# Moving the second half of m's preparation to later items, on ScalarE, VectorE and TensorE, in an attention, soft-MoE and squared-ReLU kernel

## The chip, the cores and the metric

The kernel is one program on one core of a Trainium2 chip. The metric is the device time of one execution in microseconds (us); lower is better. Times are given as the median of several executions, and one further execution is profiled, which gives the trace.

## The reference, cut to what matters

Three layers run one after the other: a chunked attention, a soft mixture of experts, and a feed-forward layer with a squared ReLU. The change lies in the last one. The output of the second layer is a product of a (3072 x 32) softmax matrix c and a (32 x 512) matrix slot_out, so the first product of the third layer can be taken as c @ (slot_out @ w_in): the small matrix m = slot_out @ w_in is computed first, and h = c @ m.

```
logits = x @ phi                               # x: 3072 x 512, phi: 512 x 32
c = softmax(logits, axis=1)
x2 = c @ slot_out                              # slot_out: 32 x 512
h = x2 @ w_in                                  # w_in: 512 x 2048, so h = c @ m, m = slot_out @ w_in
r = max(h, 0)
g = s * (r * r) + b
out = g @ w_out                                # w_out: 2048 x 512
```

## The kernel before, in words

**Items.** In the third layer the work is cut into 128 items. An item is one pair of a block of 384 rows (b) and a slice of 128 hidden columns (f). For one item TensorE computes h for the slice (`emit_h`, one 128x384 product of `cpack` with 128 columns of `mpack`, a PSUM tile of tag `s`), ScalarE applies the ReLU (L825), squares it (L829) and rounds it to a high part `ghi` (L833), VectorE takes the rest as a low part `glo` (L836), and TensorE multiplies both by the slice of w_out: six products of 512 columns with `whi` (`emit_o`, L871) and three with `wlo` (`emit_o2`, L883), which are summed in PSUM over the slices of a run. Items 0 to 15 are slices 0 to 7 of row blocks 0 and 1 in turn; items 16 to 47 are slices 0 to 15 of blocks 2 and 3 in turn. At the end of a run the sums are moved out of PSUM by L888 on ScalarE and L890 on VectorE, and the next run's first product into each of these tiles waits for that.

**Weights.** Every second item up to 46 also converts one piece of a weight (a "key", the number of the item it belongs to): ScalarE L573, then VectorE L583, L585, L587, L594, and for pieces of w_out ScalarE L792 (`whi`) and VectorE L785 and L787 (`wlo`).

**m.** `mpack` holds m in four groups of 512 columns, four slices each; its upper 64 rows are the high half, its lower 64 rows the low half. Group 0 is made ahead of the items. Groups 1, 2 and 3 are made beside items 4, 26 and 34 (`M_AT`): `emit_m` multiplies parts of slot_out by a piece of w_in (L800) and ScalarE copies the four partial sums into `mps` (L802). `emit_m2`, one item later, sums the four groups of rows with one product with `stks_all` (L806, tile `mr`, tag `s`), and `m_split` makes the two halves: ScalarE casts `mr` into `mpack` (L811), then VectorE subtracts and overwrites the low half (L812). Group 1 is first read by the h of item 8, group 2 by item 32, group 3 by item 40.

**Order.** All orders are written out by hand. The loop goes over items n; its body is, for TensorE, the h of item n, the `emit_o` of item n - 3 and the `emit_o2` of item n - 4, and only for n = 5, 6 and 7 the h stands behind these two. So the h of item 7 and the h of item 8 follow each other directly. Each engine works through its own list in order. PSUM tiles of tag `s` have two buffers, for h, for `emit_m`'s partial sums and for `mr` alike; `r2` has two, `ghi` and `glo` five.

Of the kernel before, what the change touches and what calls it, by code (L numbers as in the profile page):

```python
# [35 lines left out]
def kernel(  # L36
# [11 lines left out]
    nc = tc.nc  # L48
# [18 lines left out]
    def psum(tag, shape):  # L67
        bufs = {"s": 2, "g": 2}.get(tag, 1)
        return ps.tile(shape, F32, tag=tag, name=tag, bufs=bufs)
# [48 lines left out]
    with tc.manual_schedule():  # L118
# [447 lines left out]
        def wi_dst(t, key):  # L566
            j = key[2]
            return t[j % 2][:, :, 256 * (j // 2):256 * (j // 2) + 256]
# [6 lines left out]
        def cv_dve(key, j):  # L575
            h, lf, a, w = cv[key]
            H = w[:, :, 1]
            hi, ai = h.bitcast(I32), a.bitcast(I32)
            if key[0] == "i" and key[1] > 1 and j:
                ai = wi_dst(wis_b if key[1] % 2 else wis_a, key).bitcast(I32)  # L580
                hi, H = (x.rearrange("p (k f) -> p k f", k=2) for x in (hi, H))
            if j == 0:
                nc.vector.tensor_scalar(out=hi, in0=hi, scalar1=3, scalar2=None, op0=ALU.logical_shift_left)  # L583
            elif j == 1:
                nc.vector.scalar_tensor_tensor(out=ai, in0=H, scalar=SIGN, in1=hi, op0=ALU.bitwise_and, op1=ALU.bitwise_or)  # L585
            else:
                nc.vector.tensor_scalar(out=hi, in0=ai, scalar1=EXPM, scalar2=None, op0=ALU.bitwise_and)  # L587

        def cv_low(key, out):
            h, lf, a, w = cv[key]  # L590
            low = w[:, :, 0].bitcast(U32)
            if key[0] == "i":
                low, h = (x.rearrange("p (k f) -> p k f", k=2) for x in (low, h))
            nc.vector.scalar_tensor_tensor(out=out, in0=low, scalar=2.0 ** -52, in1=h, op0=ALU.mult, op1=ALU.mult)  # L594
# [117 lines left out]
        for i in range(16):  # L712
            emit_w2(i)
            if i == 4:
# [3 lines left out]
                mpack = pk_p.tile([128, 128 * NF], F32R, name="mpack")  # L718
# [21 lines left out]
        M_AT = (4, 26, 34)  # L740
# [24 lines left out]
        h_t, o_t = {}, {}  # L765

        def stage_a(k):
            key = cq.get(k)
            if key:
                if key[0] == "i":  # L770
                    w = wi_src(key[1], key[2])
                else:
                    w = wt[raw_of[key]].rearrange("p (f d t) -> p f d t", f=2, t=2)[:, key[1] % 2]
                cv_act(key, k // 2 % 2, w)

        def stage_d(k, j):
            key = cq.get(k)
            if key:
                h, lf, a, w = cv[key]
                if j < 3:  # L780
                    cv_dve(key, j)
                elif j == 3:
                    cv_low(key, lf if key[0] == "o" else wi_dst([wis_l[:, 0:2], wis_l[:, 2:4]], key))
                elif key[0] == "o" and j == 4:
                    nc.vector.tensor_tensor(out=a, in0=a, in1=w_hi[key[1]].bitcast(F32), op=ALU.subtract)  # L785
                elif key[0] == "o":
                    nc.vector.tensor_tensor(out=w_lo[key[1]], in0=a, in1=lf, op=ALU.add)  # L787
# [16 lines left out]
        def emit_m2(fb):  # L804
            mr = psum("s", [128, 512])
            nc.tensor.matmul(out=mr, lhsT=stks_all, rhs=mps, start=True, stop=True)  # L806
            m_split(mr, 512 * fb, slice(0, 512))

        def m_split(mp, base, cols):
            m = mpack[:, base + cols.start:base + cols.stop]  # L810
            nc.scalar.copy(out=m, in_=mp[:, cols])  # L811
            nc.vector.tensor_tensor(out=m[64:128], in0=mp[64:128, cols], in1=m[64:128].bitcast(F32), op=ALU.subtract)  # L812

        def emit_h(n):
            if n >= len(items):
                return
            (b, _, _), f = items[n]
            hq = psum("s", [128, UT])
            nc.tensor.matmul(out=hq, lhsT=mpack[:, 128 * f:128 * f + 128], rhs=cpack[:, b * UT:(b + 1) * UT],  # L819
                             start=True, stop=True)  # L820
            h_t[n] = hq

        def emit_relu(n):
            if n < len(items):
                nc.scalar.activation(out=r_g[n % 2], in_=h_t.pop(n), func=AF.Relu)  # L825

        def emit_sq(n):
            if n < len(items):
                nc.scalar.activation(out=r2_g[n % 2], in_=r_g[n % 2], func=AF.Square)  # L829

        def emit_ghi(n):
            if n < len(items):
                nc.scalar.copy(out=ghi_g[n % (LA + 2)], in_=r2_g[n % 2])  # L833
# [28 lines left out]
        def emit_o(n, parts=(0, 1)):  # L862
            r_, f = items[n]
            ghi, glo = ghi_g[n % (LA + 2)], glo_g[n % (LA + 2)]
            if f == r_[1] and 0 in parts:
                o_t[r_] = [psum(("pt", "x", "xt", "lp", "g", "g")[3 * place[r_] + t], [128, DM]) for t in range(NTU)]
            if n == len(items) - 1:
                return
            for gt in [(ghi, glo)[x] for x in parts]:
                for t in range(NTU):  # L870
                    nc.tensor.matmul(out=o_t[r_][t], lhsT=gt[:, 128 * t:128 * t + 128], rhs=w_hi[f],  # L871
                                     start=(f == r_[1] and gt is ghi), stop=False)

        def emit_o2(n):
            r_, f = items[n]
            b, f0, f1 = r_
            ghi, glo = ghi_g[n % (LA + 2)], glo_g[n % (LA + 2)]
            for t in range(NTU):
                o = o_t[r_][t]
                if n == len(items) - 1:  # L880
                    for gt in (ghi, glo):
                        nc.tensor.matmul(out=o, lhsT=gt[:, 128 * t:128 * t + 128], rhs=w_hi[f], start=False, stop=False)
                nc.tensor.matmul(out=o, lhsT=ghi[:, 128 * t:128 * t + 128], rhs=w_lo[f], start=False, stop=(f == f1 - 1))  # L883
                if f == f1 - 1:
                    if b < 4 and f0 == 0:
                        to = part[b][t] if b < 2 else os_early(b - 2, t)
                        if t == 1:
                            nc.scalar.activation(out=to, in_=o, func=AF.Copy, scale=sbt[:, 0:1])  # L888
                        else:
                            nc.vector.tensor_scalar(out=to, in0=o, scalar1=sbt[:, 0:1], scalar2=None, op0=ALU.mult)  # L890
                    else:
                        os_ = os_g[t]
                        nc.vector.scalar_tensor_tensor(out=os_, in0=o, scalar=sbt[:, 0:1], in1=part[b][t] if f0 else bias,
                                                       op0=ALU.mult, op1=ALU.add)
                        store(b, t, os_)
# [12 lines left out]
        def stages(n, *js):  # L908
            for j in js:
                stage_d(n, j)  # L910
# [44 lines left out]
        for n in range(LA + 1, len(items) + LA + 1):  # L955
            if n > 7:
                emit_h(n)
            m = n - LA - 1
            ends = 0 <= m and items[m][1] == items[m][0][2] - 1
            late = m + 1 < len(items) and m + 1 == 2 * HF + 1  # L960
            if ends or late:
                emit_o2(m)
            if 1 < m + 1 < len(items):
                emit_o(m + 1)
            if m > 1 and not ends and not late:
                emit_o2(m)
            if LA + 1 < n <= 7:
                emit_h(n)
            if n == 6:
                nc.vector.tensor_copy(out=soTb, in_=soT4[:, :, 0, :])  # L970
            emit_relu(n)
            emit_sq(n)
            stage_a(n + 1)
            emit_ghi(n)
            if n in M_AT:
                emit_m(M_AT.index(n) + 1)
            if n - 1 in M_AT:
                emit_m2(M_AT.index(n - 1) + 1)
            if LA + 1 < n <= len(items):
                emit_g(n - 1)  # L980
            stage_d(n, 1)
            stage_w(n)
            stages(n, 2, 3)
            stages(n - 1, 4, 5)
            stage_d(n + 1, 0)
            if 48 <= n < 64:
                for i in (2 * n - 96, 2 * n - 95):
                    wsum_add(i)
            if n == 64:
                colsum()  # L990
            if 65 <= n < 77:
                add_bias(n - 65)
            while wnext[0] < len(order) and last_use.get(order[wnext[0] - NRG], -1) <= n:
                load_w(1)
# [72 lines left out]
```

## Time and profile before

| | |
|---|---|
| median of 3 runs | 477.76 us (477.14 to 479.54) |
| profiled execution, its own time | 480.6 us |
| its span, first to last instruction | 478.8 us |
| mean granted TensorE clock | 0.993 |
| busy: TensorE (PE), VectorE (DVE), ScalarE (ACT) | 456.4, 308.9, 308.5 us |

Busy shares are means over very different stages. The third layer runs from about 171 us to the end, and a row of a stretch of it says more than the share over the span. In rows of a timeline, a number in brackets at the end is the idle time of that engine just before the row and what ended it.

### The profile page before, as it was taken

Reading aid. Unit: us, or ns where it says so; the run is one execution under the profiler, and the core shown is the slowest. Engines: PE = TensorE matmul, PEld = TensorE weight load, DVE = VectorE, ACT = ScalarE, POOL = GpSimd, SP = SyncE. Lnnn points to the kernel's source line nnn. Section 1 sums busy time; section 2 is a strip of 40 time slices with the busy share of each in tenths; the row PEclk is TensorE's granted clock in tenths of the full one; section 3 lists DMA queues with packets and bytes.
Section 4 is the critical chain, followed back from the end, with each engine's and each line's share of the span. In section 5 each row is a group of like instructions: output and inputs, shape, how many; then the busy total and the mean of one; then the engine's idle time right before and its main releaser. Section 6 shows DMA issues by size and latency. Waiting matters only on the chain.

```text
span 478.8 us, 10197 instructions
## 1 busy us (share of the span) xinstructions
PE 456.4 (95%) x3960; PEld 342.6 (72%) x3960; DVE 308.9 (65%) x682; ACT 308.5 (64%) x637; POOL 84.1 (18%) x154
## 2 busy tenths in 40 slices
PE   6799999999997998999999999999999999999996
PEld 5566666665543565886787888888888888888885
DVE  6778888886486767998495999975524223223232
ACT  4566666665133477998686888665766666666660
POOL 6666565550000000000000000007700000000000
PEclk8999999999998999999999999999999999999999
DMA  8999999999999932342332000003101001001011
GB/s 302 371 408 406 406 410 403 401 377 400 374 413 376 422 133 88 114 152 94 123 136 88 1 1 0 1 0 134 67 0 67 0 1 66 0 1 65 2 66 66
DMA packets 20432, 83.04 MB, mean 173 GB/s; under 512 B 2720, under 2 KB 2848, under 8 KB 14368
## 3 DMA queue, kind: packets, MB, share of 16 engines
q1 hardware_dynamic: 20384, 82.39, 44.5%
q8 instruction: 31, 0.51, 0.4%
q14 instruction: 17, 0.14, 0.1%
HBM read 76.09 MB, written 6.29 MB: 172 GB/s over the span
## 4 chain that ended last, share of the span: by engine, by line
PE 68%; DMA 12%; DVE 11%; ACT 4%; issue 2%; SPq 1%; POOL 0%; DVEq 0%; ACTq 0%; POOLq 0%
PE g L871 11%; PE lp L871 5%; PE pt L871 5%; PE x L871 5%; PE g L883 5%; PE xt L871 5%; DMA vals<-in_vm_dram 4%; DMA keys<-in_kq_dram 4%; PE s L819 4%; PE s L624 3%; PE lp L883 3%; PE pt L883 3%; PE xt L883 3%; PE x L883 3%; PE x L319 2%
## 5 line engine op out<-in xcount | busy, mean ns | idle before, releaser
L836 DVE TENSOR_TENSOR glo<-r,ghi 128x384 fp32r<-128x384 f32 x128 | 76.3, 600 | 81.5 <-ACT ghi L833 81.3
L825 ACT ACTIVATE r<-s 128x384 f32<-128x384 f32 x128 | 62.6, 489 | 51.6 <-PE s L819 51.3
L829 ACT ACTIVATE r<-r 128x384 f32<-128x384 f32 x128 | 67.2, 525 | 10.3 <-DVE glo L836 6.4
L833 ACT CAST ghi<-r 128x384 fp32r<-128x384 f32 x128 | 65.4, 511 | 3.4
L819 PE MATMUL s<-cpack,mpack 128*128 128x384 f32 x128 | 44.6, 351 | 0.2 <-DVE mpack L812 0.2
L295 ACT ACTIVATE seg<-seg 128x384 f32<-128x384 f32 x32 | 28.8, 901 | 18.9 <-DVE seg L306 15.4
L883 PE MATMUL g<-wlo,ghi 128*128 128x512 f32 x128 | 40.2, 394 | 0.0
L871 PE MATMUL g<-whi,ghi 128*128 128x512 f32 x126 | 39.6, 394 | 0.0
L871 PE MATMUL g<-whi,glo 128*128 128x512 f32 x126 | 39.4, 393 | 0.0
L858 POOL TENSOR_TENSOR keys<-keys,bias 128x512 f32<-128x512 f32 x6 | 8.4, 1434 | 165.1 <-DVE bias L847 165.1
L257 POOL TENSOR_SCALAR keys<-keys 64x416 f32<-64x416 f32 x63 | 33.6, 534 | 12.1 <-DMA keys<-in_kq_dram 5.2
L279 PE MATMUL s<-keys 128*32 128x128 f32 x768 | 29.4, 285 | 5.6 <-POOL keys L261 4.5
L319 PE MATMUL x<-vals,seg 128*32 128x128 f32 x744 | 28.3, 275 | 3.1 <-DMA vals<-in_vm_dram 2.2
L319 PEld LDWEIGHTS x<-vals,seg 128*32 128x32 f32 x744 | 20.6, 109 | 13.2 <-DVE seg L303 4.5
L819 PEld LDWEIGHTS s<-cpack,mpack 128*128 128x128 f32 x128 | 23.9, 188 | 7.9 <-issue 1.5
L883 PEld LDWEIGHTS g<-wlo,ghi 128*128 128x128 f32 x128 | 24.0, 188 | 5.2
L871 PEld LDWEIGHTS g<-whi,glo 128*128 128x128 f32 x126 | 23.7, 188 | 5.4
L279 PEld LDWEIGHTS s<-keys 128*32 128x32 f32 x768 | 19.0, 112 | 11.4 <-POOL keys L261 6.8
L313 ACT COPY seg<-pt 128x384 f32<-128x384 f32 x32 | 15.2, 475 | 18.6 <-PE pt L311 17.7
L871 PEld LDWEIGHTS g<-whi,ghi 128*128 128x128 f32 x126 | 23.7, 188 | 4.0 <-DVE vals L890 0.4
L871 PE MATMUL lp<-whi,ghi 128*128 128x512 f32 x63 | 25.5, 404 | 0.8 <-DVE vals L890 0.8
L871 PE MATMUL pt<-whi,glo 128*128 128x512 f32 x64 | 25.3, 395 | 0.7 <-DVE glo L836 0.7
(248 smaller groups left out, 991.9 us busy)
## 6 DMA issues: line engine op xcount, KB each, us to landing
seg<-in_w_dram SPq DMA_DIRECT2D x28, 1024.0 KB, 8.9
keys<-in_kq_dram SPq DMA_DIRECT2D x32, 396.0 KB, 7.4
vals<-in_vm_dram SPq DMA_DIRECT2D x64, 192.0 KB, 6.7
keys<-in_w_in_dram SPq DMA_DIRECT2D x5, 1024.0 KB, 5.0
keys<-in_w_out_dram SPq DMA_DIRECT2D x5, 1024.0 KB, 4.9
out_dram<-os SPq DMA_DIRECT2D x18, 256.0 KB, 2.1
vals<-in_w_in_dram SPq DMA_DIRECT2D x3, 1024.0 KB, 7.8
vals<-in_w_out_dram SPq DMA_DIRECT2D x3, 1024.0 KB, 4.8
```

What stands on the lines that cost most here:

```text
L257: (nc.vector if h and u == 0 else nc.gpsimd).tensor_scalar(out=stream(kz[rows, h], 0, CH), in0=k[rows, UT * h:UT * h + (NCU + 1) * CH].rea ...
L279: nc.tensor.matmul(out=o, lhsT=qt[:, 32 * c:32 * c + 32], rhs=kz[:, :, at:at + WIN], start=True, stop=not (first or last))
L295: nc.scalar.activation(out=p_r[u], in_=sm_r[u].rearrange("p t h (a r) -> p t r (h a)", a=2), func=AF.Exp, scale=scale)
L313: nc.scalar.copy(out=pts_r[u], in_=pt)
L319: nc.tensor.matmul(out=xp[32 * r:32 * r + 32, t], lhsT=pts_r[u][:, 32 * c:32 * c + 32], rhs=vbuf[u // 2 % 2][:, u % 2, :, 64 * c:64 * c + ...
L819: nc.tensor.matmul(out=hq, lhsT=mpack[:, 128 * f:128 * f + 128], rhs=cpack[:, b * UT:(b + 1) * UT], start=True, stop=True)
L825: nc.scalar.activation(out=r_g[n % 2], in_=h_t.pop(n), func=AF.Relu)
L829: nc.scalar.activation(out=r2_g[n % 2], in_=r_g[n % 2], func=AF.Square)
L833: nc.scalar.copy(out=ghi_g[n % (LA + 2)], in_=r2_g[n % 2])
L836: nc.vector.tensor_tensor(out=glo_g[n % (LA + 2)], in0=r2_g[n % 2], in1=ghi_g[n % (LA + 2)].bitcast(F32), op=ALU.subtract)
L871: nc.tensor.matmul(out=o_t[r_][t], lhsT=gt[:, 128 * t:128 * t + 128], rhs=w_hi[f], start=(f == r_[1] and gt is ghi), stop=False)
L883: nc.tensor.matmul(out=o, lhsT=ghi[:, 128 * t:128 * t + 128], rhs=w_lo[f], start=False, stop=(f == f1 - 1))
```

## The change

`emit_m2` is called two items after `emit_m` instead of one. It no longer calls VectorE: `m_split` is cut in two, `m_high` (ScalarE) stays with `emit_m2`, and `m_low` (VectorE) is called a further item later, at the end of the loop body, behind the first conversion step of the next key (`stage_d(n + 1, 0)`, L583). So `emit_m2` stands at items 6, 28 and 36 and VectorE's part at the ends of items 7, 29 and 37. The number of instructions on each engine is the same.

```diff
         def emit_m2(fb):
             mr = psum("s", [128, 512])
             nc.tensor.matmul(out=mr, lhsT=stks_all, rhs=mps, start=True, stop=True)
-            m_split(mr, 512 * fb, slice(0, 512))
+            m_high(mr, 512 * fb, slice(0, 512))
+            h_t["m", fb] = mr
+
+        def m_high(mp, base, cols):
+            nc.scalar.copy(out=mpack[:, base + cols.start:base + cols.stop], in_=mp[:, cols])
 
         def m_split(mp, base, cols):
+            m_high(mp, base, cols)
+            m_low(mp, base, cols)
+
+        def m_low(mp, base, cols):
             m = mpack[:, base + cols.start:base + cols.stop]
-            nc.scalar.copy(out=m, in_=mp[:, cols])
             nc.vector.tensor_tensor(out=m[64:128], in0=mp[64:128, cols], in1=m[64:128].bitcast(F32), op=ALU.subtract)
...
-            if n - 1 in M_AT:
-                emit_m2(M_AT.index(n - 1) + 1)
+            if n - 2 in M_AT:
+                emit_m2(M_AT.index(n - 2) + 1)
...
             stage_d(n + 1, 0)
+            if n - 3 in M_AT:
+                fb = M_AT.index(n - 3) + 1
+                m_low(h_t.pop(("m", fb)), 512 * fb, slice(0, 512))
```

In the rows that follow, numbers at a name tell buffers apart, and what stands in square brackets are the engines whose signal an instruction waits for. The lines behind the changed functions count 7 higher in the changed kernel (L812 is L819 there, L819 is L826, L836 is L843, L871 is L878, L883 is L890).

VectorE at items 4 to 7, before; the L812 is that of m's group 1, `glo4` is item 4's:

```order
L594 SCALAR_TENSOR_TENSOR seg26624_99<-keys_102,seg26624_99 128x512 [waits DVE_49]
L812 TENSOR_TENSOR mpack_2426<-s_2799,mpack_2426 64x512 [waits Activation_49]
L836 TENSOR_TENSOR glo4_2670<-r20_2659,ghi4_2665 128x384
L785 TENSOR_TENSOR seg26624_99<-seg26624_99,whi2_2623 128x512
L787 TENSOR_TENSOR wlo2_2639<-seg26624_99 128x512 [waits DVE_49]
```

The same engine in the changed kernel, from the same L594, and then the place at the end of item 7:

```order
L594 SCALAR_TENSOR_TENSOR seg26624_99<-keys_102,seg26624_99 128x512 [waits DVE_49]
L843 TENSOR_TENSOR glo4_2670<-r20_2659,ghi4_2665 128x384 [waits Activation_49]
L785 TENSOR_TENSOR seg26624_99<-seg26624_99,whi2_2623 128x512 [waits Activation_49]
...
L787 TENSOR_TENSOR wlo3_2640<-keys_102 128x512 [waits DVE_49]
L583 TENSOR_SCALAR seg26624_99<-seg26624_99 128x512 [waits Activation_49]
L819 TENSOR_TENSOR mpack_2426<-s_2818,mpack_2426 64x512
L843 TENSOR_TENSOR glo2_2668<-r21_2660,ghi2_2663 128x384 [waits PE_49,Activation_49]
```

The low half of group 1 went from ahead of item 4's `glo` to behind the L583 of key 8, past thirteen instructions, and ahead of item 7's `glo` (buffer `glo2`).

TensorE from the h of item 6 to the first product of item 5, before (`s_2816`, `s_2837` and `s_2847` are the h of items 6, 7 and 8; the L806 stands further up, ahead of item 3's products):

```order
L819 MATMUL s_2816<-cpack_2425,mpack_2426 128x384 [waits Activation_49]
L871 MATMUL pt_2722<-whi2_2623,ghi4_2665 128x512
...
L883 MATMUL g_2741<-wlo1_2638,ghi3_2664 128x512
L819 MATMUL s_2837<-cpack_2425,mpack_2426 128x384 [waits Activation_49]
L819 MATMUL s_2847<-cpack_2425,mpack_2426 128x384
L871 MATMUL lp_2739<-whi2_2623,ghi0_2661 128x512
```

The same place in the changed kernel (`s_2812`, `s_2836` and `s_2847`):

```order
L826 MATMUL s_2812<-cpack_2425,mpack_2426 128x384 [waits Activation_49]
L806 MATMUL s_2818<-mps0_2656,stk_62 128x512 [waits Activation_49]
L878 MATMUL pt_2722<-whi2_2623,ghi4_2665 128x512
...
L890 MATMUL g_2741<-wlo1_2638,ghi3_2664 128x512
L826 MATMUL s_2836<-cpack_2425,mpack_2426 128x384 [waits Activation_49]
L826 MATMUL s_2847<-cpack_2425,mpack_2426 128x384 [waits DVE_49,Activation_49]
L878 MATMUL lp_2739<-whi2_2623,ghi0_2661 128x512
```

The summing product L806 moved behind the h of item 6, and the h of item 8 now names VectorE among those it waits for.

ScalarE at items 5 to 7, before (`ghi0`, `ghi1` and `ghi2` are the high parts of items 5, 6 and 7; `s_2816` is the h of item 6):

```order
L833 CAST ghi0_2661<-r21_2660 128x384 [waits Activation_49]
L811 CAST mpack_2426<-s_2799 128x512 [waits PE_49]
L825 ACTIVATE r0_2657<-s_2816 128x384 [waits PE_49]
L829 ACTIVATE r20_2659<-r0_2657 128x384 [waits DVE_49,Activation_49]
L833 CAST ghi1_2662<-r20_2659 128x384 [waits Activation_49]
L792 CAST whi3_2624<-keys_102 128x512 [waits DMAHW2_49,DVE_49]
```

The same in the changed kernel:

```order
L840 CAST ghi0_2661<-r21_2660 128x384 [waits Activation_49]
L832 ACTIVATE r0_2657<-s_2812 128x384 [waits PE_49]
L836 ACTIVATE r20_2659<-r0_2657 128x384 [waits DVE_49,Activation_49]
L840 CAST ghi1_2662<-r20_2659 128x384 [waits Activation_49]
L811 CAST mpack_2426<-s_2818 128x512 [waits PE_49]
L792 CAST whi3_2624<-keys_102 128x512 [waits DMAHW2_49,DVE_49]
```

The cast into `mpack` moved from ahead of item 6's ReLU to behind its `ghi`.

## Rows read from the trace of the kernel before

**Rows 1.** Busy time by stretch: us, busy (instructions) of each engine, clock, DMA.

```profile
216.00:220.00 4.00, 3.16 (x13) 1.85 (x12) 3.93 (x8) 3.29 (x7) 0.00 (x0) 1.00 0.15 20
300.00:470.00 170.00, 170.00 (x752) 140.03 (x751) 71.88 (x115) 113.11 (x222) 17.46 (x12) 1.00 0.09 33
```

**Rows 2.** Whom TensorE waited for, 180 to 478 us: total, times, longest.

```profile
PE lp L871 <- DVE vals L890: 0.8, 1, 0.8
PE s L806 <- ACT mps L802: 0.8, 1, 0.8
PE pt L871 <- DVE glo L836: 0.7, 1, 0.7
```

**Rows 3.** The chain that ended last, one piece: start, length, what.

```profile
218.49 0.67 DVE vals L890
```

**Rows 4.** VectorE's timeline, items 4 to 7: start, length, instruction.

```profile
184.13 0.69 DVE L594 SCALAR_TENSOR_TENSOR seg<-keys,seg 128x512 f32<-128x512 uint32 x1
186.69 0.69 DVE L812 TENSOR_TENSOR mpack<-s,mpack 64x512 fp32r<-64x512 f32 x1 [1.88 <-ACT mpack L811]
187.40 0.56 DVE L836 TENSOR_TENSOR glo<-r,ghi 128x384 fp32r<-128x384 f32 x1
...
193.73 0.42 DVE L583 TENSOR_SCALAR seg<-seg 128x512 int32<-128x512 int32 x1
194.07 0.55 DVE L836 TENSOR_TENSOR glo<-r,ghi 128x384 fp32r<-128x384 f32 x1
```

**Rows 5.** ScalarE's timeline over the same items.

```profile
186.08 0.58 ACT L811 CAST mpack<-s 128x512 fp32r<-128x512 f32 x1
...
188.06 0.53 ACT L829 ACTIVATE r<-r 128x384 f32<-128x384 f32 x1 [0.91 <-DVE glo L836]
...
190.87 0.63 ACT L792 CAST whi<-keys 128x512 fp32r<-128x512 f32 x1 [1.74 <-DVE keys L585]
```

**Rows 6.** TensorE's timeline: items 7 and 8's h, and the product behind them.

```profile
189.51 0.51 PE L819 MATMUL s<-cpack,mpack 128*128 128x384 f32 x2
189.86 0.40 PE L871 MATMUL lp<-whi,ghi 128*128 128x512 f32 x1
```

**Rows 7.** TensorE's timeline: the h of items 18 and 19, a wait, item 21's h.

```profile
212.32 0.34 PE L819 MATMUL s<-cpack,mpack 128*128 128x384 f32 x1
...
214.58 0.34 PE L819 MATMUL s<-cpack,mpack 128*128 128x384 f32 x1
...
219.21 0.50 PE L871 MATMUL lp<-whi,ghi 128*128 128x512 f32 x1 [0.84 <-DVE vals L890]
...
220.91 0.34 PE L819 MATMUL s<-cpack,mpack 128*128 128x384 f32 x1
```

**Rows 8.** VectorE's timeline: the L583 of keys 30 and 38.

```profile
244.01 0.42 DVE L583 TENSOR_SCALAR keys<-keys 128x512 int32<-128x512 int32 x1
...
266.98 0.42 DVE L583 TENSOR_SCALAR keys<-keys 128x512 int32<-128x512 int32 x1
```

**Rows 9.** TensorE's timeline: the h of items 32 and 40.

```profile
247.97 0.34 PE L819 MATMUL s<-cpack,mpack 128*128 128x384 f32 x1
...
268.27 0.34 PE L819 MATMUL s<-cpack,mpack 128*128 128x384 f32 x1
```

**Rows 10.** TensorE's timeline in the second layer: products around its longest wait there.

```profile
147.32 1.07 PE L662 MATMUL xt<-seg,seg 128*32 128x256 f32 x16
148.32 0.66 PE L645 MATMUL lp<-ident,seg 128*128 128x128 f32 x4
...
152.72 1.12 PE L645 MATMUL lp<-ident,seg 128*128 128x128 f32 x4 [2.75 <-ACT cpack L647]
153.77 1.94 PE L662 MATMUL xt<-seg,seg 128*32 128x256 f32 x16
```

**Rows 11.** TensorE alone, short stretches there: us, busy (instructions), clock, DMA.

```profile
153.00:153.50 0.50, 0.50 (x4) 0.50 0.90 377
156.00:156.50 0.50, 0.50 (x9) 1.00 1.01 426
```

## The prediction

> **What bounds the kernel now.** I read the views in this order: whom TensorE waits for, the busy time by stretch, the chain that ended last, then the three engines' timelines around item 4. From 180 us to the end TensorE waits for another engine only three times, 2.3 us together [rows 2]: at item 5 for the summing product's input, at item 4's `glo`, and at the end of the first run, and from 300 us on it is busy in every microsecond [rows 1]. So from there on the time is TensorE's own work plus what it loses in those waits, and whatever TensorE loses or wins behind its last wait is lost or won at the end. That last wait is at 219.21 us: the first product of a new run waits for VectorE to move the old sums out (L890), and the chain runs through that L890 [rows 3]. The stretch from 216 to 220 us shows it: TensorE 3.16 of 4 us, VectorE 3.93 [rows 1]. VectorE is late there because it is full and began late: at item 5 it sat idle 1.88 us for the high half of m [rows 4].
>
> What the waits at the end of the first run cost is best read from the h of consecutive items. Items 18 and 19 are 2.26 us apart, 212.32 to 214.58, which is an item's work with no wait. Item 21 is at 220.91, where three such steps from 212.32 give 219.10. So 1.81 us are lost there [rows 7], and that is all that a faster VectorE can give back.
>
> **The change, part by part, at item 4 (group 1).**
>
> *VectorE.* The 1.88 us of idle time ahead of L812 go, and L812 goes from that place too. Item 4's `glo` starts when L594 ends, at about 184.81 (186.69 less 1.88), not at 187.40: 2.59 us earlier [rows 4]. Its inputs must be there as early. ScalarE's cast into `mpack` no longer stands ahead of item 6's ReLU, the ReLU takes its place at 186.08, and the square that waited 0.91 us for that `glo`, to 188.06, goes at about 186.6, so that `ghi` and the cast end near 188.2 and the next `whi` (190.87 before, where it waited 1.74 us for VectorE) follows VectorE's L585 at once [rows 5]. VectorE thus stays ahead by 2.59 up to the L583 of key 8: 193.73 becomes 191.14. L812 stands there now. Behind an L583 the next start comes 0.34 us later (193.73 to 194.07), so it runs from 191.48 to 192.17 [rows 4]. Item 7's `glo` then follows 2.0 us earlier than before. The work on VectorE is the same, only the wait is gone.
>
> *TensorE.* The summing product now stands behind the h of item 6, where its input is long copied; this costs nothing, and the wait that it saves lies ahead of a longer one. For the h of item 8 is the first reader of group 1's low half, and it stands directly behind the h of item 7. Before, the two ran at 189.51 as a pair, and the next product began at 189.86, so item 8's h began near 189.68 [rows 6]. Now it waits for VectorE's L812, to 192.17 plus the 0.06 us or so in which TensorE follows VectorE's eviction (218.49 plus 0.67, to 219.21 [rows 3, 7]): about 192.23. All of TensorE stands behind it: item 5's products, which need nothing from group 1, item 4's `wlo` products and item 9's h. That is 2.55 us later than before. With its waits of 0.8 and 0.7 us at items 5 and 4 gone [rows 2], and the gaps at their ends, TensorE is through with item 7's h near 188.0 and stands idle about 4.2 us.
>
> *What comes back.* VectorE is no longer late at the run's end, since it is 2.0 us ahead and TensorE 2.55 us behind; the 1.81 us of [rows 7] fall away. They can't give more: from there on TensorE is full, and its work is the same. Net of the wait: 2.55 less 1.81, a loss of 0.74 us.
>
> *The clock.* The trace holds one long wait between bursts of dense products, 2.75 us in the second layer, up to 152.72 us. The granted clock then stood at 0.50, the lower of its two levels (1.2 GHz), and came back to 1.00 (2.4 GHz) by 156 us [rows 11]. The first groups behind the wait took 1.12 and 1.94 us, where the same groups took 0.66 and 1.07 just before: 1.33 us lost [rows 10]. A wait of 4.2 us is longer, and TensorE does the bounding work behind it, so I add 1.33 us. From below the cost is 0 (the clock stays up), from above twice that, 2.7 us, if the clock stays down for two such stretches. I take one, since the nearest row shows one.
>
> The Trainium skill speaks against this change: in "TensorE: Matmul & The Clock Gate", section "HAM oscillation — how this bites in real kernels", it says that a kernel in which bursts of matmuls are parted by long waits for data has its clock throttled again and starts each burst cold. This trace agrees at 152.72 us. By that rule the loss is 0.74 plus 1.33; without it, 0.74 alone.
>
> **Items 26 and 34 (groups 2 and 3).** TensorE had no wait there: the three of [rows 2] lie elsewhere, so VectorE's waits for the cast there cost nothing, and there is nothing to win. What could be lost is the h of the first reader. Group 2 is first read by item 32's h, at 247.97 us [rows 9]. VectorE's part stands behind the L583 of key 30, which began at 244.01 [rows 8]: it ends by about 245.1, 2.9 us early. Group 3 is first read at 268.27 [rows 9]; its L583 (key 38) began at 266.98 [rows 8], so the end is at 268.0 at worst, and earlier now that VectorE doesn't wait ahead of it. Cost: 0, at most 0.1. The h between share two `s` buffers with `mr`, which holds one of them longer; their own wait is for an earlier item's ReLU, and ScalarE gets to it in time, as it does where nothing is shared [rows 2]: 0.
>
> No queue of SyncE or GpSimd is passed; weight loads keep their order, and their buffers come free earlier rather than later.
>
> **The sum.** 0.74 plus 1.33 is a loss of 2.1 us. Against the profiled execution: 478.8 us of span become 480.9, its own 480.6 become 482.7. That execution lies 2.8 us above the median of the runs shown; on the median, 477.76 becomes 479.9. That is 0.43% slower; 0.5%, about what a measurement of this kernel can tell from no change, is 2.4 us.
>
> **The rivals.**
>
> *The clock stays up (478.5).* The wait is there, but TensorE's clock doesn't fall, or falls and is up again before item 8's h. For it: the place where a low stretch begins beside the wait may shift from run to run. Against it: a shorter wait was enough at 152 us. 477.76 plus 0.74.
>
> *The clock stays down longer (slower, 481.2).* It falls early in the wait of 4.2 us and again, or stays low, behind it. This is one mechanism at item 8's h, with the price 1.33 to 2.7 us; the result is told from no change where it exceeds 1.7 us (2.4 less 0.74). For it: the wait is half as long again as that in [rows 10]. Against it: TensorE is dense behind it. 477.76 plus 0.74 plus 2.7.
>
> *TensorE does not lose at item 8 (476.0).* If VectorE reached the low half about as early as TensorE reaches item 8's h, only the gain at the run's end would be left, 1.81 us. For it: TensorE's and VectorE's loads are near each other, and VectorE's lead may be larger than 2.6 us. Against it: 4.2 us would have to go, and thirteen full instructions stand between. The change would break even with 0.74 us less of wait at a full clock.
>
> **How the numbers follow.** The forecast (one low stretch) has a chance of 0.55, the clock staying up 0.20, the longer low clock 0.17, no loss at item 8 0.08. The likeliest gives 479.9. Its own range, with a low stretch that begins partly in the wait or ends later, is 479.0 to 480.7. The range takes in the two clock rivals, 478.2 to 481.4; the last rival is left out. Slower by over 0.5% (above 480.15) come the 0.17 and about 0.13 of the forecast's 0.55, together 0.30. Faster by over 0.5% (below 475.4) needs more than the last rival's 1.81 us: 0.04. The rest, 0.66, is within 0.5%.
>
> **What would show it right or wrong.** In the profile of the changed kernel, VectorE has no long wait for ScalarE's `mpack` at item 5; TensorE has one wait of about 4.2 us for VectorE's `mpack` just ahead of the h of item 8, which becomes its longest of the third layer; the granted clock stands at 0.50 for a while from then on; and the waits for L890 at the end of the first run are gone. Item 21's h comes 0.7 us later by the walk, 2.1 us with the clock. At items 28 to 40 TensorE has no wait. I am wrong if item 8's h starts before 191 us, if the waits at L890 stay, or if TensorE waits at item 32 or 40.

## The result, and the profile after

The changed kernel takes 480.93 us (median of 12 runs, 479.55 to 484.19), the kernel before 478.19 (12 runs beside them). The ratio is 1.006, with a 95% interval of 1.0036 to 1.0084: 0.6% slower. The forecast was 2.1 us slower, the medians are 2.7 us apart, and the time lies in the range.

Whom TensorE waits for in the changed kernel from 180 to 478 us (total, times, longest) is now a single row, where [rows 2] had three:

```profile
PE s L826 <- DVE mpack L819: 4.3, 1, 4.3
```

TensorE's timeline in the changed kernel, from item 7's h (184.95) over those of items 8, 9, 10 and 11, with the first product behind item 8's, and then the h of items 18 and 21:

```profile
184.95 0.34 PE L826 MATMUL s<-cpack,mpack 128*128 128x384 f32 x1
189.54 0.66 PE L826 MATMUL s<-cpack,mpack 128*128 128x384 f32 x1 [4.25 <-DVE mpack L819]
190.00 0.63 PE L878 MATMUL lp<-whi,ghi 128*128 128x512 f32 x1
...
193.84 0.52 PE L826 MATMUL s<-cpack,mpack 128*128 128x384 f32 x1
...
196.60 0.34 PE L826 MATMUL s<-cpack,mpack 128*128 128x384 f32 x1
...
198.86 0.34 PE L826 MATMUL s<-cpack,mpack 128*128 128x384 f32 x1
...
214.68 0.34 PE L826 MATMUL s<-cpack,mpack 128*128 128x384 f32 x1
...
221.46 0.34 PE L826 MATMUL s<-cpack,mpack 128*128 128x384 f32 x1
```

Three things are to be seen. Item 8's h waits 4.25 us for VectorE. Behind it items 8 and 9 take 4.30 and 2.76 us, and only from item 10 on an item takes 2.26. And from item 18 to item 21 there are 6.78 us, three times 2.26: the waits at the end of the first run, which cost 1.81 us in [rows 7], are gone.

Why items 8 and 9 are slow is in the busy time of TensorE by stretch (us, busy with instructions, granted clock, DMA share, GB/s):

```profile
187.00:188.00 1.00, 0.00 (x0) 1.00 0.22 49
188.00:189.00 1.00, 0.00 (x0) 0.56 0.71 246
190.00:191.00 1.00, 1.00 (x4) 0.50 0.70 295
193.00:194.00 1.00, 1.00 (x4) 0.50 0.00 0
195.00:196.00 1.00, 1.00 (x6) 1.00 0.00 0
```

The clock fell to the lower of its two levels, 1.2 GHz, late in the wait (near 188.1 us) and stayed there until about 194.9 us. The first product behind item 8's h takes 0.63 us in the timeline above, where the same product takes 0.40 in [rows 6]. From item 8's h to item 10's are 7.06 us; less twice 2.26, the fall cost 2.54 us in this execution.

VectorE's timeline in the changed kernel answers to [rows 4]: no wait between L594 and item 4's `glo`, and the low half (L819) behind the L583 of key 8.

```profile
181.32 0.69 DVE L594 SCALAR_TENSOR_TENSOR seg<-keys,seg 128x512 f32<-128x512 uint32 x1
181.93 0.55 DVE L843 TENSOR_TENSOR glo<-r,ghi 128x384 fp32r<-128x384 f32 x1
...
188.25 0.42 DVE L583 TENSOR_SCALAR seg<-seg 128x512 int32<-128x512 int32 x1
188.70 0.69 DVE L819 TENSOR_TENSOR mpack<-s,mpack 64x512 fp32r<-64x512 f32 x1
189.43 0.56 DVE L843 TENSOR_TENSOR glo<-r,ghi 128x384 fp32r<-128x384 f32 x1
```

**Reading the two executions side by side.** The span grew only from 478.8 to 479.4 us, since this profiled execution came to the third layer earlier: L594 starts at 181.32 here and at 184.13 in [rows 4], 2.81 us. Most of that is the second layer, where the same wait for `cpack` was shorter and was not followed by a slow clock:

```profile
150.41 0.66 PE L645 MATMUL lp<-ident,seg 128*128 128x128 f32 x4 [1.32 <-ACT cpack L647]
150.99 1.07 PE L662 MATMUL xt<-seg,seg 128*32 128x256 f32 x16
```

In [rows 10] the wait was 2.75 us and the groups behind it ran at half speed. The change doesn't touch that place, so the two executions are laid against each other at L594. Item 8's h then comes 2.67 us later than in [rows 6] (189.54 plus 2.81, less 189.68), item 21's h 3.36 us later than in [rows 7] (221.46 plus 2.81, less 220.91). The terms give the same: 2.67 of wait, plus 2.54 of clock, less 1.81 that came back, is 3.40.

The question for the runs is what is wait and what is clock in the 2.7 us of the medians. My theory is that both hang on the place of VectorE's low half, which holds up item 8's h and all of TensorE's queue behind it. The rivals are the sum's place, the late groups, and VectorE's or ScalarE's order.

### The profile page after: what moved, and what is told of

The parts are those of the page before. It is cut to its first block, busy times and chain, and to the rows that moved or that the text cites. A ratio compares the mean times of both kernels' runs of the same rounds, so it can differ in the third digit from the quotient of the medians.

```text
span 479.4 us, 10201 instructions
## 1 busy us (share of the span) xinstructions
PE 456.4 (95%) x3960; PEld 344.4 (72%) x3960; DVE 310.2 (65%) x682; ACT 309.3 (65%) x637; POOL 84.2 (18%) x154
## 4 chain that ended last, share of the span: by engine, by line
PE 72%; DMA 10%; DVE 8%; ACT 4%; POOL 2%; issue 2%; SPq 1%; DVEq 0%; POOLq 0%; ACTq 0%
PE g L878 12%; PE lp L878 6%; PE pt L878 6%; PE x L878 6%; PE g L890 6%; PE xt L878 6%; PE s L826 5%; DMA seg<-in_w_dram 4%; DMA vals<-in_vm_dram 3%; PE s L624 3%; PE pt L890 3%; PE xt L890 3%; PE x L890 3%; PE lp L890 3%; DMA keys<-in_kq_dram 3%; PE x L319 2%
## 5 line engine op out<-in xcount | busy, mean ns | idle before, releaser
L843 DVE TENSOR_TENSOR glo<-r,ghi 128x384 fp32r<-128x384 f32 x128 | 76.3, 600 | 82.0 <-ACT ghi L840 81.7
L836 ACT ACTIVATE r<-r 128x384 f32<-128x384 f32 x128 | 67.2, 525 | 5.8 <-DVE glo L843 1.6
L826 PE MATMUL s<-cpack,mpack 128*128 128x384 f32 x128 | 45.2, 355 | 4.5 <-DVE mpack L819 4.5
L890 PE MATMUL g<-wlo,ghi 128*128 128x512 f32 x128 | 40.2, 394 | 0.0
L878 PE MATMUL g<-whi,ghi 128*128 128x512 f32 x126 | 39.9, 397 | 0.0
L878 PE MATMUL g<-whi,glo 128*128 128x512 f32 x126 | 39.8, 397 | 0.0
L826 PEld LDWEIGHTS s<-cpack,mpack 128*128 128x128 f32 x128 | 24.2, 190 | 12.3 <-issue 6.6
L878 PEld LDWEIGHTS g<-whi,glo 128*128 128x128 f32 x126 | 24.0, 190 | 5.5
L890 PEld LDWEIGHTS g<-wlo,ghi 128*128 128x128 f32 x128 | 24.0, 188 | 5.2
L878 PEld LDWEIGHTS g<-whi,ghi 128*128 128x128 f32 x126 | 23.9, 190 | 3.6 <-DVE mpack L819 0.4
L878 PE MATMUL pt<-whi,ghi 128*128 128x512 f32 x64 | 26.2, 409 | 0.1
L890 PE MATMUL pt<-wlo,ghi 128*128 128x512 f32 x64 | 25.6, 400 | 0.2 <-DVE wlo L787 0.2
```

What stands on the lines that cost most here:

```text
L843: nc.vector.tensor_tensor(out=glo_g[n % (LA + 2)], in0=r2_g[n % 2], in1=ghi_g[n % (LA + 2)].bitcast(F32), op=ALU.subtract)
```

## Experiments

Each was timed against the kernel before on the chip that it ran on. The kernel before has a median of 478.50 us beside the first four and of 478.34 beside the others, so runs are compared by their ratios first. VectorE's move of the old sums out of PSUM, L890 in the kernel before, is L897 in the changed kernel.

**The wait filled with work.** Extra products go into item 8's own PSUM tile, ahead of its h, which overwrites them.

```diff
             hq = psum("s", [128, UT])
+            for _ in range(16 if n == 8 else 0):
+                nc.tensor.matmul(out=hq, lhsT=mpack[:, 0:128], rhs=cpack[:, 0:UT], start=True, stop=True)
```

> The changed kernel, with 16 extra products of 384 columns (about 2.7 us at the full clock) put on TensorE into item 8's own PSUM tile ahead of its h, which overwrites them. They need no part of m's group 1, so VectorE's low half comes as late as before and item 8's h starts as late. My theory (wait 0.74 us net, the rest of the loss is the clock behind it): the granted clock stays at 1.00 from the wait on, items 8 and 9 take 2.3 us each and not 4.3 and 2.8, and the time is about 0.7 us above the kernel before (ratio 1.0015), some 2 us below the changed kernel. Rival (the whole loss is the wait, the clock costs nothing): as the changed kernel, ratio 1.006.

Measured: 478.79 us, ratio 1.0011 (0.9995 to 1.0028). TensorE's timeline: the extra products (L827), then the h of items 8, 9 and 10 (L828).

```profile
186.69 3.07 PE L827 MATMUL s<-cpack,mpack 128*128 128x384 f32 x16 [1.17 <-ACT r L834]
189.70 0.44 PE L828 MATMUL s<-cpack,mpack 128*128 128x384 f32 x1
...
192.05 0.34 PE L828 MATMUL s<-cpack,mpack 128*128 128x384 f32 x1
...
194.31 0.34 PE L828 MATMUL s<-cpack,mpack 128*128 128x384 f32 x1
```

Its busy time in the second in which item 8's products run:

```profile
190.00:191.00 1.00, 1.00 (x6) 1.00 0.93 393
```

Item 8's h starts as late as in the changed kernel (8.13 us behind L594, 8.22 there), yet items 8 and 9 take 2.35 and 2.26 us, the clock is at 1.00, and 2.1 us are back (480.93 to 478.79; 2.3 by the ratios). The intervals of the two ratios don't overlap. So the clock is most of the loss, and what the wait alone costs, net of what comes back, is the 0.1% that is left, which is not clear of zero.

**Groups 2 and 3 alone.** Group 1 is made as in the kernel before.

```diff
-            if n - 2 in M_AT:
+            if n == 5:
+                emit_m2(1)
+                m_low(h_t.pop(("m", 1)), 512, slice(0, 512))
+            if n - 2 in M_AT[1:]:
...
-            if n - 3 in M_AT:
+            if n - 3 in M_AT[1:]:
```

> The change at items 26 and 34 alone; group 1 is summed and halved beside item 5 as in the kernel before. My theory: groups 2 and 3 cost and bring nothing, ratio 1.000, and TensorE waits in its rows as in the kernel before (at items 5 and 4 and at the end of the first run). Rival (the late groups hold up the h that share the PSUM buffers, or the first reader of their columns): ratio above 1.002, with a wait of TensorE between 236 and 272 us.

Measured: 478.04 us, ratio 0.9993 (0.9973 to 1.0013). Whom TensorE waits for in its third layer:

```profile
PE lp L878 <- DVE vals L897: 0.9, 1, 0.9
PE s L806 <- ACT mps L802: 0.8, 1, 0.8
PE pt L878 <- DVE glo L843: 0.7, 1, 0.7
```

These are the three of [rows 2]; none is at items 26 to 40. The late groups cost and bring nothing that these times can tell.

**The low half earlier.** As the changed kernel, but VectorE's part stands behind the second conversion step (L585) of item 6.

```diff
             stage_d(n, 1)
+            if n - 2 in M_AT:
+                fb = M_AT.index(n - 2) + 1
+                m_low(h_t.pop(("m", fb)), 512 * fb, slice(0, 512))
...
-            if n - 3 in M_AT:
-                fb = M_AT.index(n - 3) + 1
-                m_low(h_t.pop(("m", fb)), 512 * fb, slice(0, 512))
```

> The summing product two items behind as in the changed kernel, but VectorE's low half one item earlier, behind the second conversion step of item 6's key (L585), where ScalarE's cast has just ended. My theory (both the wait and the clock hang on where the low half stands): item 8's h waits about 1 us instead of 4.3, starts 0.7 us earlier than in the kernel before, the clock stays up, the waits for L890 shrink, and the time is 2.0 to 2.5 us below the kernel before: ratio 0.995. Rival (the sum being an item later costs by itself, or VectorE is held up by the low half there as it was before): ratio 1.000 or above.

Measured: 476.26 us, ratio 0.9962 (0.9942 to 0.9982). TensorE's timeline, the h of items 7, 8 and 9:

```profile
186.16 0.33 PE L826 MATMUL s<-cpack,mpack 128*128 128x384 f32 x1
187.35 0.45 PE L826 MATMUL s<-cpack,mpack 128*128 128x384 f32 x1 [0.87 <-DVE mpack L819]
...
189.72 0.34 PE L826 MATMUL s<-cpack,mpack 128*128 128x384 f32 x1
```

VectorE's, around the low half:

```profile
185.86 0.68 DVE L585 SCALAR_TENSOR_TENSOR keys<-keys 128x512 int32<-128x512 int32 x1
186.60 0.69 DVE L819 TENSOR_TENSOR mpack<-s,mpack 64x512 fp32r<-64x512 f32 x1
187.33 0.43 DVE L587 TENSOR_SCALAR keys<-keys 128x512 int32<-128x512 int32 x1
```

VectorE finds its input ready there and waits for nothing, TensorE waits 0.87 us and not 4.25, and the kernel is faster than both, 0.4% below the kernel before (1.8 us, where 2.0 to 2.5 were expected). Only the place of VectorE's part differs from the changed kernel.

**The sum's place alone.** The kernel before, with `emit_m2` and its `m_split` two items behind.

```diff
-            if n - 1 in M_AT:
-                emit_m2(M_AT.index(n - 1) + 1)
+            if n - 2 in M_AT:
+                emit_m2(M_AT.index(n - 2) + 1)
```

> One part of the change alone: the summing product two items behind, with VectorE's low half directly behind it as in the kernel before (ahead of item 5's glo). My theory: VectorE waits about 1.2 us for the cast there instead of 1.9 and is 0.8 us ahead of the kernel before, item 8's h waits about 1 us and is 0.7 us ahead, the waits for L890 stay, and the time is 0.8 us below the kernel before: ratio 0.998. Rival (the sum's place is the cost): ratio 1.003 or above.

Measured: 477.07 us, ratio 0.9975 (0.9959 to 0.9992). Whom TensorE waits for (lines as in the kernel before):

```profile
PE lp L871 <- DVE vals L890: 0.9, 1, 0.9
PE s L819 <- DVE mpack L812: 0.8, 1, 0.8
```

VectorE's timeline, its wait for the cast:

```profile
187.35 0.69 DVE L812 TENSOR_TENSOR mpack<-s,mpack 64x512 fp32r<-64x512 f32 x1 [1.12 <-ACT mpack L811]
```

The sum two items behind is a small gain, not the cost. VectorE still waits 1.12 us, and the wait for L890 at the run's end stays, as the theory had it.

**The low half's place alone.** The sum one item behind as before, VectorE's part at the end of item 7.

```diff
-            if n - 2 in M_AT:
-                emit_m2(M_AT.index(n - 2) + 1)
+            if n - 1 in M_AT:
+                emit_m2(M_AT.index(n - 1) + 1)
```

> The other part of the change alone: the summing product one item behind as in the kernel before, VectorE's low half at the end of item 7 as in the changed kernel. My theory: item 8's h starts as late as in the changed kernel, TensorE's wait there is shorter (about 3.3 us) only because its wait of 1 us for the sum's input at item 5 is back; the waits for L890 are gone; net 0.7 us of wait plus the clock, ratio 1.004 to 1.006. Rival (the two parts make the loss together): clearly below the changed kernel, ratio 1.002 or less.

Measured: 480.52 us, ratio 1.0052 (1.0031 to 1.0072). TensorE's timeline, the h of items 8, 9 and 10:

```profile
189.41 0.41 PE L826 MATMUL s<-cpack,mpack 128*128 128x384 f32 x1 [3.48 <-DVE mpack L819]
...
192.66 0.52 PE L826 MATMUL s<-cpack,mpack 128*128 128x384 f32 x1
...
195.54 0.34 PE L826 MATMUL s<-cpack,mpack 128*128 128x384 f32 x1
```

Its granted clock, in the stretches behind item 8's h (us, busy with instructions, clock, DMA share, GB/s):

```profile
190.00:191.00 1.00, 1.00 (x6) 0.81 0.59 238
191.00:192.00 1.00, 1.00 (x4) 0.50 0.00 0
```

This part makes the loss, with or without the other. In this execution the clock fell behind the start of item 8's products, and the two items took 6.13 us, 1.61 more than twice 2.26.

**Item 8's h behind work that doesn't need it.** The changed kernel, with that h behind item 5's products and item 4's `wlo` products.

```diff
-            if n > 7:
+            if n > 8:
                 emit_h(n)
...
-            if LA + 1 < n <= 7:
+            if LA + 1 < n <= 8:
                 emit_h(n)
```

> The changed kernel, with item 8's h behind item 5's products and item 4's wlo products (as it is written for items 5 to 7), so that nine products that need nothing of group 1 no longer stand behind the wait. My theory (the loss is what is queued behind the waiting h): TensorE does these 2.1 us of work in the wait, which falls to about 2.1 us, the waits for L890 stay away, and at a full clock the time is 1.4 us below the kernel before, ratio 0.997; a wait of 2.1 us may still cost some of the clock, then up to 1.000. Rival (VectorE's or ScalarE's order, not TensorE's queue, sets the loss): as the changed kernel, 1.006.

Measured: 477.96 us, ratio 0.9983 (0.9960 to 1.0006). TensorE's timeline, items 8 and 9's h as a pair, and item 10's:

```profile
188.92 0.58 PE L826 MATMUL s<-cpack,mpack 128*128 128x384 f32 x2 [2.18 <-DVE mpack L819]
...
191.41 0.34 PE L826 MATMUL s<-cpack,mpack 128*128 128x384 f32 x1
```

TensorE's clock in the wait:

```profile
187.00:188.00 1.00, 0.00 (x0) 1.00 0.57 164
```

VectorE's low half is as late as in the changed kernel (7.38 us behind L594 in both), and the loss is gone: what was queued behind the waiting h set it. In this execution the clock stayed at 1.00 through the wait, so the run takes away both parts of the loss at once, the wait and the slow clock; it is the filled wait that parts them. Against a clock at full speed throughout (0.997) some tenths of a microsecond are missing in the median; whether the clock falls at item 8 in some of the other runs isn't shown.

**Both.** The early low half, and item 8's h behind that work.

> The early low half (behind item 6's second conversion step) and item 8's h behind item 5's products, together. My theory: no wait is left at item 8, but from there VectorE is the later one at the end of the first run, where a wait for L890 of about 1.2 us comes back: no faster than the early low half alone, ratio 0.995 to 0.997. Rival (TensorE's queue is still the bound there): faster than the early low half by the 0.9 us of its wait, ratio 0.994.

Measured: 476.12 us, ratio 0.9957 (0.9938 to 0.9977), the same as the early low half alone. Its only wait of TensorE in the third layer:

```profile
PE lp L878 <- DVE vals L897: 0.9, 1, 0.9
```

With no wait left at item 8, the wait at the end of the first run is back (0.9 us, where about 1.2 were expected): there VectorE sets the time again. The two bounds lie within a microsecond of each other.

**A longer wait.** The changed kernel, with two more VectorE additions ahead of the low half.

```diff
+                for _ in range(2 if n == 7 else 0):
+                    c0 = cpack[:, 0:512].bitcast(F32)
+                    nc.vector.tensor_tensor(out=os_g[0], in0=c0, in1=c0, op=ALU.add)
                 m_low(h_t.pop(("m", fb)), 512 * fb, slice(0, 512))
```

> The changed kernel with two extra VectorE additions (128x512, 1.35 us together, into a tile that is overwritten later) ahead of the low half of group 1. My theory (item 8's h sets the end): TensorE's wait grows from 4.3 to 5.6 us and the time by 1.35 us against the changed kernel, ratio to the kernel before 1.008 to 1.009. Rival (VectorE has slack there and the loss is the clock alone): no slower than the changed kernel, 1.006.

Measured: 482.36 us, ratio 1.0084 (1.0053 to 1.0115). TensorE's timeline, the h of items 8, 9 and 10:

```profile
190.86 0.66 PE L826 MATMUL s<-cpack,mpack 128*128 128x384 f32 x1 [5.55 <-DVE mpack L819]
...
195.16 0.52 PE L826 MATMUL s<-cpack,mpack 128*128 128x384 f32 x1
...
197.83 0.34 PE L826 MATMUL s<-cpack,mpack 128*128 128x384 f32 x1
```

The wait grew by 1.30 us and the time by 1.4 by the medians, 1.1 by the ratios (0.0024 of 478): what is added ahead of the low half is added to the end. The intervals of this run and of the changed kernel overlap, so the slope is borne out by the trace more than by the times. The slow clock isn't what grew: items 8 and 9 take 6.97 us here and 7.06 in the changed kernel.

**One measure for all.** What an execution lost or won before the third layer drops out if one counts from the start of the L594 of [rows 4] to the h of item 21, behind the last wait. The rows are in each run's trace; the last column is the ratio turned into microseconds.

| kernel | L594 | item 21's h | between | against before | by the times |
|---|---|---|---|---|---|
| before | 184.13 | 220.91 | 36.78 | | |
| changed | 181.32 | 221.46 | 40.14 | +3.36 | +2.9 |
| the wait filled | 181.57 | 219.16 | 37.59 | +0.81 | +0.5 |
| groups 2 and 3 alone | 181.77 | 218.55 | 36.78 | 0.00 | -0.3 |
| the low half earlier | 182.51 | 217.36 | 34.85 | -1.93 | -1.8 |
| the sum's place alone | 183.26 | 219.31 | 36.05 | -0.73 | -1.2 |
| the low half's place alone | 181.19 | 220.40 | 39.21 | +2.43 | +2.5 |
| item 8's h behind work | 180.70 | 216.26 | 35.56 | -1.22 | -0.8 |
| both | 182.63 | 217.48 | 34.85 | -1.93 | -2.1 |
| a longer wait | 181.33 | 222.67 | 41.34 | +4.56 | +4.0 |

Each row is one execution, and it agrees with the times of all its runs within 0.6 us. It parts the loss: 0.81 us are the wait, net of what came back, and 2.55 (40.14 less 37.59) the clock of that execution.

## Why the prediction was right, point by point

- **VectorE's idle time goes.** Right: no wait at item 5, item 4's `glo` follows L594 at once.
- **Item 8's h waits.** Right in place and size: 4.25 us of wait where about 4.2 were forecast, 2.67 us of delay where 2.55 were. That TensorE's queue behind it carries the loss is shown by putting that h behind nine products: 4.25 us of wait become 2.18, and 1.006 becomes 0.998.
- **What comes back at the end of the first run.** Right: 1.81 us; three items there take 6.78 us, three times 2.26, so no wait is left there that could give more.
- **The net of the wait, 0.74 us.** Borne out by the trace, 0.81 us with the wait filled, and not contradicted by the times: 0.1%, 0.5 us of 478.5, with an interval from nothing to 1.3 us.
- **The clock.** The mechanism was right, and the term was mis-sized. The step that failed is "I take one, since the nearest row shows one": I took 1.33 us from the one low stretch of [rows 10], and the profiled execution lost 2.54, near the upper bound of 2.7. The low level lasted from about 188.1 to 194.9 us there, twice as long as in the execution that gave the price (152.3 to 155.7 us), so this execution is the slower rival's. It isn't so in every one: with the low half's place alone the low level lasted from about 190.6 to 194.0 us and cost 1.61, and three of the changed kernel's twelve runs have that execution's mean clock, 0.995, where the profiled one has 0.985. Those three are no faster than the rest (480.36 to 481.40 us), so the clock's share in each run stays open.

  In the medians the clock costs 2.1 us (480.93 less 478.79); the two intervals together leave about 1 to 3.7, which is clear of zero but not of 1.33. So the 0.6% measured lies between the forecast of 0.4% and its slower rival, and its interval, 0.36% to 0.84%, takes in the forecast too. The largest chance, 0.66, was on a change within 0.5%.
- **The rule on bursts and waits.** The work behind a long wait began at the slow clock, and filling the wait gave 2.1 us back. The Trainium skill, "TensorE: Matmul & The Clock Gate", section "HAM oscillation — how this bites in real kernels", had that sign. These runs agree with it for the waits of 3.48, 4.25 and 5.55 us; the wait of 2.18 us, with the clock at 1.00, shows that not every wait brings it.
- **Groups 2 and 3.** Right: 0.9993.
- **The rival that TensorE loses nothing at item 8.** It fell as a description of this change. The early low half comes to about its price, 0.9962 where 1.81 us (0.4%) were worked out, but by another sum, so that the match is in part luck: item 8's h comes 0.71 us earlier against L594 (4.84 us, 5.55 before), which the rival left out, and only 1.28 of the 1.81 us come back at the end of the first run (items 18 to 21 take 7.31 us, 210.05 to 217.36).

## What to carry to other kernels

A later place for an instruction relieves the engine that waited for its input, and moves the wait to the first reader; ask what stands behind that reader in its own in-order queue, and whether it needs the result. The best of the places tried was the first at which the input is ready without a wait, not the last before the reader. A wait on the engine that sets the time can have a second price, the clock behind it, which here was larger than the wait's net cost (2.55 us and 0.81); it can be seen by filling the wait with work.

## What I had not expected of the hardware

The length of a wait did not tell whether the clock falls. In front of item 8, 2.18 us left it at 1.00 (item 8's h behind other work), but a shorter wait in the second layer, in the run with the sum's place alone, was followed by the low level. TensorE's timeline there, and its busy time:

```profile
151.71 0.82 PE L645 MATMUL lp<-ident,seg 128*128 128x128 f32 x4 [1.99 <-ACT cpack L647]
152.46 1.94 PE L662 MATMUL xt<-seg,seg 128*32 128x256 f32 x16
152.50:153.00 0.50, 0.50 (x9) 0.50 0.90 377
```

Nor did it tell how much is lost: after waits of 3.48, 4.25 and 5.55 us the two items behind lost 1.61, 2.54 and 2.45 us. Each of these is one execution; how they spread over runs was not measured.
